# The layout of batch 0's inverse spectrum before its transposition by identity matmuls: strided or contiguous weight columns

## The chip, the cores and the metric

The kernel runs on one core of a Trainium2 chip. The metric is the device time of one execution in microseconds (us). The names are those of the profile: PE is TensorE's matmuls, PEld its weight loads (they overlap the matmuls: 432.1 and 322.8 us busy in a span of 441.9), DVE is VectorE, ACT ScalarE, POOL GpSimd. "Clock" is the share of TensorE's full clock that was granted, as the profile records it. "L617" is line 617 of the kernel; the change shortens the file by three lines, so L617 and L629 become L615 and L626 after it, and L660, L671, L704, L737, L740, L798, L1003, L1018 become L657, L668, L701, L734, L737, L795, L1000, L1015. ACT's evacuation stays L587.

In the kernel a matmul names a stationary operand, the weights, for which the profile has a weight load (LDWEIGHTS) of its own, and a moving operand. Its result goes to a PSUM tile (`ps` in the profile); an "evacuation" is the copy from there by ACT or DVE into a tile in SBUF, from which later matmuls read.

## The reference

A spectral layer and then a two-layer MLP whose weights are chosen per batch item:

```python
X = np.fft.rfft(x, axis=1)                    # x: 8 x 2496 x 256
Yr = Xr @ w_r - Xi @ w_i + b_r                # and Yi likewise
Yr = np.sign(Yr) * np.maximum(np.abs(Yr) - 0.01, 0.0)
y = np.fft.irfft(Yr + 1j * Yi, n=2496, axis=1)
# ... (one expert per batch item, from the mean of y)
h = np.maximum(y @ w1[e], 0.0); out = gate * (h @ w2[e])
```

The transforms are two-stage: 2496 = 39 x 64, so there are 64-point stages on 128 partitions and 39-point stages on 117 or 120. Between the two inverse stages the data changes its layout: 20 frequencies k and 128 positions n = (g, q), six q to each of 22 groups g, have to become 22 tiles with the 120 pairs (k, q) on partitions. Batches 1 to 7 do this through DRAM. Batch 0, which nothing can hide, does it on chip: it keeps the spectrum with channels on partitions and transposes it with 44 identity matmuls (22 groups, two channel halves). This change is about those.

## The kernel before

The instructions of all engines are emitted in an order that a small list scheduler in the kernel fixes when it is built. PE's instructions come in that order in the timelines, and while one waits no later one runs: in the last experiment below PE stood idle for 2.68 us before its first identity matmul.

The evacuation of the first inverse stage (L587) puts batch 0's spectrum into one tile `A`, for each half h as `(k, q, g)` with g innermost; positions 126 and 127 of each k go to a small zero-padded region, `first["r"]`, which serves as group g = 21.

```python
def add_inverse_b0(q, i0, n, cell, oy, vt):
    # ... matmuls L576: the 64-point inverse stage of n frequencies, into a PSUM pair
    def ev(eng):
        pv = hc["p"].rearrange("p h (k n) -> p h k n", k=n)
        k0 = 4 * q + i0
        COPY[eng](out=first["V"][:, :, 126 * k0 : 126 * (k0 + n)].rearrange(   # L587
            "p h (k q g) -> p h k q g", k=n, q=6),
            in_=pv[:, :, :, 0:126].rearrange("p h k (g q) -> p h k q g", q=6))
        COPY[eng](out=first["r"][...], in_=pv[:, :, :, 126:P])                # L591
```

The turn then takes four groups at a time (L617). The stationary operand of each matmul is 120 columns of `A`, 21 elements apart; the moving operand is the 128-column identity.

```python
def add_turn(v_ops, vt):
    for gq in range(6):
        gs = range(4 * gq, min(4 * gq + 4, NG))
        tag = "oh"[gq % 2]              # two PSUM pairs, used in turn
        def mm(_, ...):
            for i, g in enumerate(gs):
                for ch in range(2):
                    c0 = D * i + P * ch
                    nc.tensor.matmul(                                          # L617
                        pt[0:120, c0 : c0 + P],
                        first["V"][:, ch, g : g + 2500 : 21]
                        if g < 21 else first["r"][:, ch], eye)
        # ... evacuation of the pair to V2 by ACT or DVE (L629)
```

Between the six groups the scheduler puts the last inverse stage of batch 0 (L1003, evacuated by L1018) and work of batch 1 (L704, L737, L740). After the last of them comes L798, the first matmul of batch 2; from there on PE has work all the time. In what follows "the turn" is the stretch from the first identity matmul to the first L798 (L795 after the change).

## Time and profile before

| | before |
|---|---|
| time, median of 3 runs | 442.82 us (441.03 to 443.32) |
| the profiled execution | 443.56 us, span 441.9 us, mean clock 0.988 |
| the turn in it | 36.74 to 54.74 us: 18.00 us |

From the page of the profiled execution: the span, each engine's busy time (share of the span), the clock in 40 slices, in tenths, and the share of each engine in the chain of work that ended last.

```profile
span 441.9 us, 9430 instructions
...
PE 432.1 (98%) x3572; PEld 322.8 (73%) x3572; DVE 302.0 (68%) x616; ACT 333.1 (75%) x643; POOL 33.5 (8%) x54
...
PEclk9998699999999999999999999999999999999999
...
PE 92%; DMA 2%; DVE 2%; ACT 1%; SPq 1%; issue 1%; POOL 0%; ACTq 0%; POOLq 0%
```

PE sets the pace. The fourth and fifth slices of the clock line show the one flaw, at 33 to 55 us: 8 and 6 tenths. The table of windows for stretches of the turn and for all that follows it:

```profile
core 0: us, PE busy (x) PEld busy (x) DVE busy (x) ACT busy (x) POOL busy (x), PEclk, DMA share, GB/s
36.74:54.74 18.00, 17.57 (x113) 15.24 (x109) 7.35 (x8) 9.24 (x11) 0.00 (x0) 0.72 0.39 54
39.34:42.75 3.41, 3.41 (x14) 2.46 (x14) 0.66 (x1) 1.33 (x2) 0.00 (x0) 0.50 0.91 139
42.75:46.17 3.42, 3.42 (x25) 3.42 (x25) 1.23 (x1) 1.63 (x2) 0.00 (x0) 1.00 0.05 8
46.17:52.99 6.82, 6.82 (x44) 5.59 (x42) 3.05 (x3) 3.47 (x4) 0.00 (x0) 0.50 0.00 1
54.74:441.91 387.17, 383.55 (x3222) 289.12 (x3221) 274.28 (x553) 300.33 (x598) 23.00 (x34) 1.00 0.76 179
```

The window that follows the turn has PE busy for 383.55 of 387.17 us at full clock, so the end follows the start of that window, and what shortens the turn shortens the kernel. In the turn the clock is 0.50 in two stretches, 39.34 to 42.75 and 46.17 to 52.99 us: 3.41 us and twice that.

Next the weight loads of the turn, as the timeline shows them (start, duration of the merged group, engine, line, operation, operands, shapes, count):

```profile
36.69 1.85 PEld L617 LDWEIGHTS <-A 128*120 128x120 f16 x8
...
38.65 1.85 PEld L617 LDWEIGHTS <-A 128*120 128x120 f16 x8
...
44.19 1.86 PEld L617 LDWEIGHTS <-A 128*120 128x120 f16 x8
```

Eight loads take 1.85 us. A single one is recorded with 319 ns (median), so their spacing is about (1.85 - 0.32) / 7 = 0.22 us. The starts of the individual records say 222 ns. A matmul of 128 columns whose weights are ready needs only about 56 ns: eight L576 matmuls take 0.45 us in the chain. So in these groups PE has always something in flight, but by this estimate it computes only for 56 / 222, a quarter, of the time.

The same stretch on PE; the two groups below at 40.49 and 48.44 us ran at half clock:

```profile
36.74 1.94 PE L617 MATMUL ps<-eye,A 128*120 128x128 f16 x8
...
40.49 1.91 PE L704 MATMUL ps<-w,XB 128*128 128x512 f16 x4
...
48.44 0.99 PE L1003 MATMUL ps<-wi,V 120*128 120x117 f16 x8
...
50.94 0.73 PE L617 MATMUL ps<-eye,A 128*120 128x128 f16 x4
...
54.74 0.38 PE L798 MATMUL ps<-xin,wa 117*120 117x512 f16 x1 [0.43 <-ACT ysb L1018]
```

### The profile page before, as it was taken

To read this page: it belongs to the slowest core of one execution; us is meant where nothing else is said; L and a number is where in the kernel's file an instruction comes from. 1 tells how busy PE (TensorE), PEld (TensorE's weight loads), DVE (VectorE), ACT (ScalarE), POOL (GpSimd) and SP (SyncE) were. 2 spreads that over 40 slices of the span, in tenths; PEclk is the share of its full clock that TensorE was granted. 3 is DMA by queue.
4 is the path that set the end of the run, shared out by engine and by line. 5 is a ranking of instruction groups with operands and counts; after the bars stand their busy time and mean duration, and the time that the engine had idled before them with its cause. 6 is when DMAs were issued, how large, how long until landed. Compare 5 with 4: busy or idle time off the path is not lost.

```text
span 441.9 us, 9430 instructions
## 1 busy us (share of the span) xinstructions
PE 432.1 (98%) x3572; PEld 322.8 (73%) x3572; DVE 302.0 (68%) x616; ACT 333.1 (75%) x643; POOL 33.5 (8%) x54
## 2 busy tenths in 40 slices
PE   6999999999999999999999999999999999999996
PEld 2568866778777787778777787778777787777775
DVE  1484577487877869676877869677877869613662
ACT  3586598778777788667876788777876787778884
POOL 3230010020000210020000210020000010000000
PEclk9998699999999999999999999999999999999999
DMA  8899048979997799949987799959988368432122
GB/s 176 219 167 152 3 85 225 244 190 200 142 282 234 145 202 223 271 132 218 168 238 243 154 232 192 250 157 215 195 222 241 121 123 160 146 97 89 49 96 92
DMA packets 85605, 77.20 MB, mean 175 GB/s; under 512 B 7610, under 2 KB 72398, under 8 KB 85560
## 3 DMA queue, kind: packets, MB, share of 16 engines
q1 hardware_dynamic: 68366, 57.73, 47.5%
q0 software_dynamic: 16880, 18.46, 27.5%
q8 instruction: 28, 0.46, 0.4%
q10 hardware_dynamic: 314, 0.41, 0.3%
q14 instruction: 17, 0.14, 0.1%
HBM read 57.54 MB, written 37.49 MB: 215 GB/s over the span
## 4 chain that ended last, share of the span: by engine, by line
PE 92%; DMA 2%; DVE 2%; ACT 1%; SPq 1%; issue 1%; POOL 0%; ACTq 0%; POOLq 0%
PE ps L1305 30%; PE ps L1342 29%; PE ps L900 9%; PE ps L1045 4%; PE ps L529 3%; PE ps L798 3%; PE ps L704 3%; PE ps L862 3%; PE ps L1224 2%; PE ps L617 2%; DMA xin<-in_x_dram 2%; PE ps L737 1%; DMA ti<-d_ti 1%; PE ps L740 1%; PE ps L1003 1%; DVE z L752 1%
## 5 line engine op out<-in xcount | busy, mean ns | idle before, releaser
L1317 ACT ACTIVATE hs<-ps 128x512 f16<-128x512 f32 (+1 forms) x293 | 168.2, 594 | 68.2 <-PE ps L1305 64.2
L1305 PE MATMUL ps<-ysb,w1s 128*128 128x512 f16 (+1 forms) x640 | 178.2, 374 | 0.0
L1342 PE MATMUL ps<-w2s,hs 128*128 128x256 f16 x1152 | 162.3, 272 | 0.1
L1342 PEld LDWEIGHTS <-hs 128*128 128x128 f16 x1152 | 110.9, 98 | 42.7 <-issue 0.2
L1305 PEld LDWEIGHTS <-w1s 128*128 128x128 f16 x640 | 68.6, 113 | 18.6 <-issue 0.2
L914 DVE TENSOR_TENSOR tt<-ps,bias 128x512 f16<-128x512 f32 x60 | 38.6, 686 | 24.5 <-PE ps L900 24.5
L942 DVE TENSOR_TENSOR Y<-z,cl 64x512 f16<-64x512 f16 x120 | 50.4, 420 | 2.8
L900 PE MATMUL ps<-w,XT 128*128 128x256 f16 x360 | 49.4, 273 | 0.0
L1359 ACT ACTIVATE ost<-ps,gbc 128x512 f32<-128x512 f32 x65 | 44.7, 688 | 2.3 <-PE ps L1342 2.3
L900 PEld LDWEIGHTS <-XT 128*128 128x128 f16 x360 | 35.2, 98 | 7.7
L923 DVE TENSOR_TENSOR z<-ps,tt 128x512 f16<-128x512 f32 x60 | 38.4, 681 | 0.1
L808 ACT CAST A<-ps 120x512 f16<-120x512 f32 x48 | 29.5, 614 | 7.2 <-PE ps L798 6.8
L1061 DVE CAST ysb<-ps 128x468 f16<-128x468 f32 (+1 forms) x24 | 15.0, 630 | 25.6 <-PE ps L1045 25.5
L1061 ACT CAST ysb<-ps 128x468 f16<-128x468 f32 (+1 forms) x60 | 28.0, 523 | 3.2 <-PE ps L1045 2.6
L870 DVE CAST XT<-ps 128x512 f16<-128x512 f32 x24 | 16.5, 688 | 16.0 <-PE ps L862 16.0
L536 ACT CAST V<-ps 128x512 f16<-128x512 f32 x45 | 26.2, 609 | 0.0
L798 PE MATMUL ps<-xin,wa 117*120 117x512 f16 x66 | 23.1, 380 | 0.4 <-ACT ysb L1018 0.4
L1045 PE MATMUL ps<-wi,V 120*128 120x117 f16 (+1 forms) x308 | 22.4, 214 | 0.0
L870 ACT CAST XT<-ps 128x512 f16<-128x512 f32 x36 | 22.0, 615 | 0.0
L704 PE MATMUL ps<-w,XB 128*128 128x512 f16 x80 | 21.8, 404 | 0.1
L529 PE MATMUL ps<-Y,ti 128*128 128x256 f16 x140 | 21.8, 272 | 0.0
L536 DVE CAST V<-ps 128x512 f16<-128x512 f32 x25 | 17.2, 688 | 6.4 <-PE ps L529 5.4
(104 smaller groups left out, 438.4 us busy)
## 6 DMA issues: line engine op xcount, KB each, us to landing
out_dram<-ost SPq DMA_DIRECT2D x72, 256.0 KB
xin<-in_x_dram POOLq DMA_DIRECT2D x21, 429.0 KB, 11.7
scr<-V SPq DMA_DIRECT2D x35, 256.0 KB
XB<-fwd SPq DMA_DIRECT2D x30, 256.0 KB
V<-scr SPq DMA_DIRECT2D x14, 504.0 KB
fwd<-A SPq DMA_DIRECT2D x18, 360.0 KB
w1s<-in_moe_w_dram POOLq DMA_DIRECT2D x8, 512.0 KB, 7.4
w2s<-in_moe_w_dram POOLq DMA_DIRECT2D x8, 512.0 KB, 8.0
```

The lines of the kernel that those rows point to most:

```text
L536: COPY[eng](out=hc["V"][:, n * u : n * u + n].rearrange("p i c -> p (i c)"), in_=hc["p", u])
L870: COPY[eng](out=cell["X"][:, ch, :, 0:2].rearrange("p a r i k -> p a i r k"), in_=hc["p"].rearrange("p (a i r k) -> p a i r k", a=2, i=2, ...
L900: nc.tensor.matmul(pm[:, D * a : D * a + D], cell["X"][:, ch, a, t].rearrange("p i k -> p (i k)"), w4[:, ch, t, :], start=(ch == 0), stop= ...
L914: nc.vector.tensor_add(out=cell["tt"][:, r], in0=cell["T", 2].rearrange("p (a c) -> p a c", a=2), in1=bias[:, r].unsqueeze(1).to_broadcast ...
L923: nc.vector.tensor_add(out=cell["z"][:, r], in0=cell["T", 1 - r].rearrange("p (a c) -> p a c", a=2), in1=cell["tt"][:, r])
L942: nc.vector.tensor_sub(out=Y[64 * r : 64 * r + 64, :, i], in0=cell["z"][s, r], in1=cell["cl"][s, r])
L1045: nc.tensor.matmul(pi[:, 117 * i : 117 * i + M], V2[:, g, ch * P : ch * P + P], w)
L1061: COPY[eng](out=yv[:, :, 12 * gb : 12 * gb + 3 * nf].rearrange("p a (g j) -> p a g j", j=3), in_=pi[:, 0 : 117 * nf].rearrange("p (g a j) ...
L1305: nc.tensor.matmul(ph[:, 0:nl], w1v[:, ch, fc // 4, :, fc % 4], ysb_t[b][:, ch, ns : ns + nl], start=(ch == 0), stop=(ch == 1))
L1317: nc.scalar.activation(out=o, in_=i, func=AFT.Relu)
L1342: nc.tensor.matmul(oc["p"][:, i, :], cell["hs"][:, ft, s0 : s0 + P], w2s_t[b][:, ft, :], start=(ft == 0), stop=(ft == E - 1))
L1359: nc.scalar.activation(out=ost, in_=oc["p"], func=AFT.Copy, scale=gbc_t[b])
```

## The change

The evacuation now writes each group's 120 columns next to each other: layout `(g, k, q)` with q innermost, and group 21 as one more g. The loads become contiguous. The evacuation reads PSUM contiguously and writes runs of six fp16 values (12 bytes) 240 bytes apart; before it wrote runs of 504.

```diff
-                first["V"] = A[:, 0 : 252 * NK1].rearrange(
-                    "p (h m) -> p h m", h=2)
-                first["r"] = A[:, 252 * NK1 : 264 * NK1].rearrange(
-                    "p (h m) -> p h m", h=2)
-                nc.vector.memset(A[:, 252 * NK1 : 264 * NK1], 0.0)
+                first["V"] = V = A[:, 0 : 240 * NG].rearrange(
+                    "p (h g k q) -> p h k g q", h=2, g=NG, q=6)
+                first["T"] = A[:, 0 : 240 * NG].rearrange(
+                    "p (h g m) -> p h g m", h=2, g=NG)
+                nc.vector.memset(V[:, :, :, 21], 0.0)
...
-            COPY[eng](out=first["V"][:, :, 126 * k0 : 126 * (k0 + n)].rearrange(
-                "p h (k q g) -> p h k q g", k=n, q=6),
-                in_=pv[:, :, :, 0:126].rearrange(
-                "p h k (g q) -> p h k q g", q=6))
-            COPY[eng](out=first["r"][:, :, 6 * k0 : 6 * (k0 + n)].rearrange(
-                "p h (k q) -> p h k q", k=n)[:, :, :, 0:2],
-                in_=pv[:, :, :, 126:P])
+            COPY[eng](out=first["V"][:, :, k0 : k0 + n, 0:21],
+                      in_=pv[:, :, :, 0:126].rearrange(
+                          "p h k (g q) -> p h k g q", q=6))
+            COPY[eng](out=first["V"][:, :, k0 : k0 + n, 21, 0:2],
+                      in_=pv[:, :, :, 126:P])
...
-                            first["V"][:, ch, g : g + 2500 : 21]
-                            if g < 21 else first["r"][:, ch], eye)
+                            first["T"][:, ch, g], eye)
```

No computing instruction is added or dropped, and their order on every engine is the same.

## The prediction

> **What bounds the kernel now.** From about 56 us on PE never stops: the table of windows shows it 100% busy at clock 1.00. The end follows the start of that dense run, the first L798 matmul (54.74 us in the timeline). From 36.74 to there runs batch 0's tail: six groups of identity matmuls (L617, 44 in all), in fixed PE order with L1003, L704, L737/740. The chain of waits there is almost all PE, 10 us of it L617.
>
> **Why L617 is slow.** Its weight loads take 319 ns (median), one every 222 ns, at full and half clock alike; their columns lie 42 bytes apart. Loads with contiguous columns take 98 ns (128 columns) and 133 ns (120 columns, L798). A control: the last two weights (g=21) are contiguous already; their spacing is 80 to 107 ns at half clock. [...]
>
> **Second cost.** Slow loads leave PE computing a quarter of the time, and the granted clock falls to 0.50 at 39.2 to 42.7 and 46.2 to 53.0 us. There four L704 matmuls cost 1.71 instead of 0.86 us (twice), eight L1003 0.79 instead of 0.42. [...]the trace's steps are 3.41 us.
>
> **What the change does.** Removes the stride from 42 of 44 loads; instruction counts and order stay. It moves the scatter to ACT's evacuation L587: PSUM read becomes contiguous, SBUF writes become runs of 6 fp16 (12 bytes) 240 bytes apart, formerly 504 contiguous.
>
> **Sum (estimates from the durations above).** Spacing 222 to about 56 ns: 42 x 0.166 = 7.0 us of PE. Clock staying at 1.0: about 3 us more. Given back: PE then waits for evacuations (two pairs of banks; 1.0 us on ACT, 1.2 on DVE) and for the shared rings. Replaying the fixed order with these durations, L798 starts near 46.1: 8.6 us gained, bounded at the end by ACT's evacuations of L1003.
> Cost: ACT evacuations with short scattered runs are slower in this trace: runs of 3 elements (39 of them) cost 0.37 us against 0.26 expected by count, single elements 0.39 against 0.19, about 5 ns per jump; runs of 12 cost nothing. Runs of 6 last 5 ns, so just about hidden[...]. I give 20% to a clock drop remaining (costs 1 to 3 us).
> Net gain: about 7.7 us, all on the critical path, as PE runs dense afterwards.
>
> **Prediction: 435.0 us, 8 in 10 between 432.8 and 438.0.** Faster by over 2% (below 433.96): 0.27; within 2%: 0.72; slower: 0.01.
>
> **What would show it.** L617 loads near 133 ns, spacing near 56; window 36 to 47 at clock 1.00; L617's part of the chain about 2.5 us, not 10; first L798 near 46 to 47.5; PE waits released by ACT or DVE evacuations; L587 1.0 to 1.4 us; from L798 to the end unchanged (387 us).
>
> **What would make it wrong.** Scattered writes slower than 1.4 us; the clock dropping anyway; L798's input landing after 46 us (it landed about 44 to 45).

The sum came to about 7.7 us net: 7.0 us from the loads and about 3 from the clock, of which the replay with its waits left 8.6, less the costs weighed by their chances. One of these costs: a slower evacuation L587 (about 1 us, at 35%). The 0.9 us between 8.6 and 7.7 contains that term, and the 1.4 us among the criteria was its upper end. That the slow loads lower the clock was the estimate here; an experiment below tests it.

## The result, and the profile after

| | before | after |
|---|---|---|
| first comparison, median | 442.07 us (441.03 to 443.32, 4 runs) | 435.67 us (435.40 to 435.87, 4 runs) |
| ratio, 95% interval | | 0.9854 (0.9823 to 0.9885) |
| repeated with more rounds, median | 443.06 us (440.91 to 444.98, 11 runs) | 435.53 us (435.30 to 435.81, 6 runs) |
| ratio, 95% interval | | 0.9833 (0.9804 to 0.9862) |

A ratio here is the mean time of one kernel's fast runs over that of the other's of the same rounds, so it is not quite the ratio of the medians in the table. The gain is 1.5 to 1.7%, clear of noise and short of 2%.

The page after, the same lines:

```profile
span 434.1 us, 9428 instructions
...
PE 423.7 (98%) x3572; PEld 314.9 (73%) x3572; DVE 301.9 (70%) x616; ACT 332.7 (77%) x643; POOL 33.1 (8%) x54
...
PEclk9999999999999999999999999999999999999999
...
PE 93%; DVE 3%; ACT 2%; issue 1%; ACTq 0%
```

The clock line has no dip any more. The weight loads of the turn:

```profile
37.38 0.52 PEld L615 LDWEIGHTS <-A 128*120 128x120 f16 x8
...
38.23 0.52 PEld L615 LDWEIGHTS <-A 128*120 128x120 f16 x8
...
40.66 0.52 PEld L615 LDWEIGHTS <-A 128*120 128x120 f16 x8
```

Eight loads in 0.52 instead of 1.85 us; one takes 133 ns, and the spacing of the individual records is 56 ns, that of the matmuls themselves. PE in the turn:

```profile
37.43 0.61 PE L615 MATMUL ps<-eye,A 128*120 128x128 f16 x8
...
38.98 1.04 PE L701 MATMUL ps<-w,XB 128*128 128x512 f16 x4
...
42.22 0.58 PE L1000 MATMUL ps<-wi,V 120*128 120x117 f16 x8
...
43.66 0.39 PE L615 MATMUL ps<-eye,A 128*120 128x128 f16 x4
...
46.86 0.38 PE L795 MATMUL ps<-xin,wa 117*120 117x512 f16 x1 [0.43 <-ACT ysb L1015]
```

The turn starts at 37.43 and ends at 46.86 us, 9.43 us long instead of 18.00. (It started 0.69 us later than in the profiled execution of before. That shift stands already at 21 us, before the first changed instruction: an ACT cast that began at 21.01 us in the one began at 21.70 in the other, and near 9 us DVE had waited 7.87 instead of 7.16 us for the first input. It belongs to the execution, not to the change.) The windows:

```profile
core 0: us, PE busy (x) PEld busy (x) DVE busy (x) ACT busy (x) POOL busy (x), PEclk, DMA share, GB/s
37.43:46.86 9.43, 8.63 (x112) 6.90 (x109) 7.25 (x8) 8.75 (x11) 0.00 (x0) 1.00 0.78 99
46.86:434.10 387.24, 383.57 (x3222) 289.13 (x3221) 274.31 (x553) 300.43 (x598) 22.67 (x34) 1.00 0.74 179
```

The rest of the kernel takes 387.24 us, where it took 387.17: nothing was given back later. But in the turn PE now has pauses. The chain of waits has pieces of ACT and DVE between those of PE (start, length, what):

```profile
37.63 0.46 ACT XB L668
38.09 0.40 issue
38.49 0.44 ACT XB L668
...
43.82 0.24 PE ps L615 x4
44.06 0.02 issue
44.08 0.70 DVE V L626
...
45.42 0.43 PE ps L1000 x8
45.85 0.02 issue
45.87 0.95 ACT ysb L1015
```

In the profiled execution of before, the only such piece in the turn was the last one, ACT's evacuation L1018, for which the first L798 waits (0.43 us). But that execution was slowed by its clock: in the one at full clock that is shown below, the chain has DVE's piece of 0.70 us as well. New with the fast loads are only the two pieces of ACT's L668.

The evacuation L587 that now scatters its writes, before and then after (count, duration in ns as min/median/max, first and last start, shapes):

```profile
L587 ACT CAST A<-ps x6: 578/1002/1054, 23.3 to 35.8; 128x1008 f16<-128x1008 f32 x4, 128x504 f16<-128x504 f32 x2
```

```profile
L587 ACT CAST A<-ps x6: 690/1020/1077, 24.0 to 36.4; 128x1008 f16<-128x1008 f32 x4, 128x504 f16<-128x504 f32 x2
```

### The profile page after: what moved, and what is told of

Its sections match the earlier page's. It is cut to its first block, busy times and chain, and to the rows that moved or that the text cites. A ratio compares the mean times of both kernels' runs of the same rounds, so it can differ in the third digit from the quotient of the medians.

```text
span 434.1 us, 9428 instructions
## 1 busy us (share of the span) xinstructions
PE 423.7 (98%) x3572; PEld 314.9 (73%) x3572; DVE 301.9 (70%) x616; ACT 332.7 (77%) x643; POOL 33.1 (8%) x54
## 4 chain that ended last, share of the span: by engine, by line
PE 93%; DVE 3%; ACT 2%; issue 1%; ACTq 0%
PE ps L1302 31%; PE ps L1339 29%; PE ps L897 9%; PE ps L1042 4%; PE ps L529 4%; PE ps L795 3%; PE ps L859 3%; PE ps L701 3%; PE ps L1221 2%; PE ps L441 2%; DVE z L749 1%; PE ps L734 1%; PE ps L657 1%; PE ps L737 1%; DVE Y L764 1%
## 5 line engine op out<-in xcount | busy, mean ns | idle before, releaser
L867 DVE CAST XT<-ps 128x512 f16<-128x512 f32 x24 | 16.5, 688 | 16.0 <-PE ps L859 16.0
L795 PE MATMUL ps<-xin,wa 117*120 117x512 f16 x66 | 23.1, 380 | 0.4 <-ACT ysb L1015 0.4
L1042 PEld LDWEIGHTS <-V 120*128 120x128 f16 x308 | 19.8, 98 | 2.4
```

Of the source, the lines that this page charges most:

```text
L867: COPY[eng](out=cell["X"][:, ch, :, 0:2].rearrange("p a r i k -> p a i r k"), in_=hc["p"].rearrange("p (a i r k) -> p a i r k", a=2, i=2, ...
L1042: nc.tensor.matmul(pi[:, 117 * i : 117 * i + M], V2[:, g, ch * P : ch * P + P], w)
```

## The experiments

Seven kernels. The theory, an estimate from the profile of before: the gain has two parts, the loads themselves (PE waits for weights, one load every 222 ns) and the clock (it falls to 0.50 because PE waits). The rivals: the clock is only a symptom; or the scatter of the kernel before has another source, so that the clock part was misread.

### The kernel before once more

No edit.

> The unchanged kernel once more, to see its own scatter. Theory 'clock phase': [...]its executions differ (441.0 to 443.3 us so far) and the longer ones have the lower mean granted clock; ratio 1.00, another profile with the half-clock stretches begun at another point of the turn and the turn (first L617 to first L798) 16.5 to 18.5 us long. Rival 'input landing': the scatter is in the first 20 us (landing of x), and the turn is 18.0 us again to 0.1 us.

Measured: 443.08 us median (440.95 to 444.46, 6 runs), ratio 1.0008 (0.9975 to 1.0042). The profiled execution was the fastest of the six, 440.95 us, and in it the clock never fell:

```profile
36.72 1.94 PE L617 MATMUL ps<-eye,A 128*120 128x128 f16 x8
...
40.46 1.03 PE L704 MATMUL ps<-w,XB 128*128 128x512 f16 x4
...
47.34 0.58 PE L1003 MATMUL ps<-wi,V 120*128 120x117 f16 x8
...
48.62 0.55 PE L617 MATMUL ps<-eye,A 128*120 128x128 f16 x4
...
51.99 0.38 PE L798 MATMUL ps<-xin,wa 117*120 117x512 f16 x1 [0.43 <-ACT ysb L1018]
```

```profile
36.72:51.99 15.27, 14.64 (x112) 13.53 (x109) 7.35 (x8) 9.12 (x11) 0.00 (x0) 1.00 0.47 59
```

The first fence is PE in the turn, the second the window of the turn. The same program, the same loads, but L704 at 40.46 takes 1.03 instead of 1.91 us, L1003 at 47.34 takes 0.58 instead of 0.99, and the turn is 15.27 us long instead of 18.00. The profiles agree up to the first group's start (36.72 and 36.74 us). So the turn missed my 16.5 to 18.5 us: I had expected the dips to move, and in this execution there was none at all. What holds of the theory is that the longer executions are those with the lower clock, as the table below shows. The half-clock stretches can lie differently: the longer one begins at 46.17 us in before, and at about 44.6 us in the second kernel with other steps below, which is the same up to the turn (there the group of L1002 at 44.57 takes 0.97 us, where the one at 42.49 takes 0.58). What decides where they lie and how many there are is not shown.

For 25 executions of before the mean granted clock is on record (the 11 of these rounds, these six, seven of the experiments, and the first profiled one). One stretch of 3.41 us at half clock lowers the mean over 442 us by 0.5 x 3.41 / 442 = 0.004; the profiled execution, with three times 3.41 us at 0.50, has a mean of 0.988. By this estimate the recorded clock tells how many such stretches there were, from none in the first line to four in the last:

| mean clock | executions | time, mean (range) |
|---|---|---|
| 0.999 to 1.000 | 6 | 441.3 us (440.91 to 442.00) |
| 0.995 | 4 | 442.2 us (442.05 to 442.45) |
| 0.991 to 0.992 | 5 | 443.4 us (443.06 to 444.00) |
| 0.988 | 9 | 444.0 us (443.56 to 444.98) |
| 0.983 | 1 | 444.46 us |

The rival "input landing" explains a scatter of 0.7 us or so in the first 37 us of the profiles, not this order of 3 us by clock.

### The strided loads with a busier PE

```diff
                     c0 = D * i + P * ch
+                    w = (512 - c0 % 512) // P
                     nc.tensor.matmul(
-                        pt[0:120, c0 : c0 + P],
+                        pt[0:120, c0 : c0 + P * w].rearrange("p (w c) -> p w c", w=w),
                         first["V"][:, ch, g : g + 2500 : 21]
-                        if g < 21 else first["r"][:, ch], eye)
+                        if g < 21 else first["r"][:, ch],
+                        eye.unsqueeze(1).to_broadcast([P, w, P]))
```

> Strided weights as before, but every identity matmul streams 1 to 4 copies of the identity (320 columns on average), whose extra output is overwritten by the next ones; result right. Spacing stays 222 ns, PE computes about 60% of it instead of 25%. Theory 'two costs': the clock stays at 1.00 in the turn and about 3 us of the gain come without touching the loads: 438.5 to 440 us, ratio about 0.993. Rival 'the loads are all': the clock is a symptom and worth nothing: ratio 1.000. If the clock falls all the same, the run tells nothing.

Measured: 441.49 us median (441.25 to 441.80, 6 runs), result right, ratio 0.9966 (0.9936 to 0.9996). The recorded clock was 0.999 to 1.000 in all six, where before in the same rounds ranged from 0.988 to 1.000. Its turn, at full clock:

```profile
37.47:52.95 15.48, 14.70 (x112) 13.69 (x109) 7.35 (x8) 9.13 (x11) 0.00 (x0) 1.00 0.47 60
```

This answers two questions. Adding useless columns, and nothing else, stops the dips (0.999 or more in all six, where 8 of the 11 executions of before had 0.988 to 0.995), so in these runs the dips came from how little PE computed while it waited for weights; and stopping them makes the kernel faster on average, by just more than the noise, and takes away its scatter. The clock is not a mere symptom. But the gain is 1.5 us (0.34%), not the 3 us that I had put down, because only some executions of before had lost 3 us. The turn is as long as that of the undisturbed execution of before (15.48 and 15.27 us): the strided loads alone keep it there.

### The contiguous loads with the old evacuation

```diff
-                            first["V"][:, ch, g : g + 2500 : 21]
+                            first["V"][:, ch, 120 * g : 120 * g + 120]
                             if g < 21 else first["r"][:, ch], eye)
```

The result is wrong: the loads read whatever 120 neighbours lie there.

> The evacuation of before (contiguous writes), but the identity matmuls read 120 contiguous columns of it: wrong data on purpose. Theory 'the loads are the whole gain and the scattered writes cost nothing': the same time as the changed kernel within 0.3 us (about 435.6). Rival 'the writes take a part back': 0.5 to 1.5 us faster than the changed kernel, L587 at 1.00 us against 1.02.

Measured: 435.28 us median (435.08 to 435.84, 6 runs), ratio 0.9830 (0.9800 to 0.9859). L587 has a median of 1.00 us here, and the turn takes 9.43 us, exactly as in the changed kernel. So the gain is in the loads. No cost of the scattered writes is shown: the two medians differ by 0.25 us, and the ranges of the two kernels overlap. (The old evacuation also reads PSUM with a step of six values, which the new one does not; the runs compare both together.)

### The changed kernel in the same rounds

> The changed kernel in the same rounds, as the mark for the others: ratio 0.985 (0.982 to 0.988), turn 9.4 us, clock 1.00, spread of its runs under 1 us where before has 2 us.

Measured: 435.53 us median (435.30 to 435.81, 6 runs), ratio 0.9833 (0.9804 to 0.9862), turn 37.05 to 46.48 us (9.43 us), clock 0.999 to 1.000 in all six. As expected; the scatter of before is gone.

### Which steps between columns are slow

Two kernels with before's evacuation, where each of the six groups of loads reads its columns with another step (the edit is abbreviated). Wrong results on purpose, and one look each (437.95 and 442.14 us, single executions that mix the steps; only the durations of the loads are used).

```diff
-                            first["V"][:, ch, g : g + 2500 : 21]
-                            if g < 21 else first["r"][:, ch], eye)
+                            first["V"][:, ch, g % 16 : g % 16 + 119 * s[gq] + 1 : s[gq]], eye)
                             # s = (2, 3, 4, 5, 8, 16) in one, (6, 7, 9, 10, 12, 20) in the other
```

> Before's evacuation; the six groups of identity matmuls read weights whose 120 columns lie 2, 3, 4, 5, 8, 16 fp16 apart (4, 6, 8, 10, 16, 32 bytes), one step a group; wrong data on purpose. [...] Rival 'any step is slow': about 222 ns at every step. Rival 'the cost grows with the distance': under 222 ns at step 8 and 16.

> The same with steps 6, 7, 9, 10, 12, 20 (12 to 40 bytes). [...] Any step is slow: all 222. Grows with the distance: a rise from 9 to 20.

The weight loads of the first of the two kernels, eight each with steps 2, 3, 4, 5 and 8, and, as the last line, the eight with step 12 of the second:

```profile
37.10 0.54 PEld L617 LDWEIGHTS <-A 128*120 128x120 f16 x8
...
37.95 0.76 PEld L617 LDWEIGHTS <-A 128*120 128x120 f16 x8
...
39.35 1.07 PEld L617 LDWEIGHTS <-A 128*120 128x120 f16 x8
...
40.77 1.19 PEld L617 LDWEIGHTS <-A 128*120 128x120 f16 x8
...
42.30 1.83 PEld L617 LDWEIGHTS <-A 128*120 128x120 f16 x8
...
45.24 1.78 PEld L617 LDWEIGHTS <-A 128*120 128x120 f16 x8
```

The usual spacing of the loads in a group, from the starts of the individual records (step 1 from the changed kernel, step 21 from before):

| step, fp16 | 1 | 2 | 3 | 4 | 5 | 6 | 7 | 8 | 9 | 10 | 12 | 16 | 20 | 21 |
|---|---|---|---|---|---|---|---|---|---|---|---|---|---|---|
| bytes | 2 | 4 | 6 | 8 | 10 | 12 | 14 | 16 | 18 | 20 | 24 | 32 | 40 | 42 |
| spacing, ns | 56 | 56 | 85 | 111 | 140 | 167 | 193 | 220 | 213 | 206 | 209 | about 220 | 212 to 218 | 222 |

The two fall in the form in which I wrote them: "any step is slow" falls at step 2 (56 ns), "grows with the distance" falls above step 8 (220 ns there, 206 to 222 beyond). What fits these groups is simpler: up to step 8, columns 16 bytes apart, the spacing grows in proportion to the step, and beyond it stays about the same. A price of 27.6 ns per step gives 83, 110, 138, 166, 193, 221 ns for s = 3 to 8, within 3 ns of the usual spacings in the table. At step 2 it gives 55 ns, just hidden behind the matmul's 56. That price is a fit to these groups, not something the trace records, and what causes it is not shown. Why steps 9 to 12 are a few per cent under the plateau stays open. In before the spacing of the loads was the same at full and at half clock (median 222 ns in the group at 44.19 us, 223 in the one at 46.58), so here it did not follow the granted clock.

### Writes without runs

The changed kernel with (q, k) for (k, q) in the 120 columns, and the rows of the inverse table in the same order, so that the result is right and the loads are contiguous:

```diff
-    wi0 = wi.transpose(1, 0, 2).reshape(120, 117)
+    wi0 = wi.reshape(120, 117)
...
-                    "p (h g k q) -> p h k g q", h=2, g=NG, q=6)
+                    "p (h g q k) -> p h k g q", h=2, g=NG, q=6)
```

> The changed kernel, with the 120 columns of a weight in the other order (q slow, k fast) and the inverse table to match: result right, loads contiguous as in the changed kernel (56 ns), but ACT's evacuation writes single fp16 values 40 and 240 bytes apart instead of runs of 6. Theory 'ACT pays about 5 ns per jump, hidden under runs of 6': L587 about 5 us for 1008 elements instead of 1.02, and the kernel 10 to 16 us slower than the changed one (445 to 452 us). Rival 'scattered writes are free for ACT here': L587 1.0 us and 435.5 us.

Measured: 453.14 us median (453.02 to 453.29, 4 runs), ratio 1.0221 (1.0189 to 1.0252): slower than before, though unclear at 2%, because the interval lies on both sides of it. By the medians it is 17.6 us slower than the changed kernel, more than the 10 to 16 us expected. It was run at another time. The evacuation, and the start of the turn (L590 is the second copy of the same evacuation):

```profile
L587 ACT CAST A<-ps x6: 2383/4580/4616, 23.8 to 50.3; 128x1008 f16<-128x1008 f32 x4, 128x504 f16<-128x504 f32 x2
...
53.08 1.11 PE L615 MATMUL ps<-eye,A 128*120 128x128 f16 x8 [2.68 <-ACT A L590]
```

4.58 us instead of 1.02 for 1008 values. A copy of 1024 values takes 1.01 us on ACT and one of 512 takes 0.61, so 0.2 us are fixed and a value costs 0.78 ns; here it costs (4.58 - 0.2) / 1008 = 4.3 ns. The turn starts at 53.08 us, 16 us later than in the changed kernel, because PE waits for these evacuations, and while it waits the clock falls too (mean 0.976 to 0.981), which my estimate had left out: the turn begins at half clock and takes 11.11 us, to 64.19 us, instead of 9.43. So the loads could have been made contiguous in a way that loses more than it gains. By these numbers runs of six are just long enough: 1008 values in runs of six are 168 jumps, 168 x 4.3 ns = 0.72 us, less than the 0.79 us (1008 x 0.78 ns) that ACT needs for the values anyway. That the jumps hide behind the values in this way is an estimate from these durations. A copy in runs of three that every one of these kernels has agrees with it: 234 values (the last of L1018, 78 runs) take 0.52 us, where the values alone would give 0.2 + 234 x 0.78 ns = 0.38 us and the jumps 0.2 + 78 x 4.3 ns = 0.54.

## Why the prediction was right

It said 435.0 us, 432.8 to 438.0, with 72% for "within 2%"; measured were 435.67 and 435.53 us, 1.5 to 1.7% faster.

- **What bounds the kernel.** Right. The part after the turn took 387.17 us before and 387.24 after, and the gain is that of the turn.
- **The loads.** Right, also in size. Spacing 222 to 56 ns, 133 ns for one. Undisturbed by the clock, the turn went from 15.27 to 9.43 us: 5.84 us. The 42 loads that lost their stride would account for 42 x 0.166 = 6.97 us. Two of them, each the first after a group of L704, were hidden before already (in the undisturbed execution their matmuls are followed by the next after 59 ns), so 40 x 0.166 = 6.64 us could be gained; the other 0.8 us became pauses of PE.
- **The pauses.** Right. The replay of the fixed order gave 46.1 - 36.74 = 9.4 us for the turn; measured are 9.43. The chain shows ACT's and DVE's evacuations as the releasers, though DVE's was there before at full clock too. In these 9.43 us ACT is busy for 8.75 and DVE for 7.25 us, so that a still faster PE would probably gain little here; no run tested that.
- **The clock.** Right that it would stay up (0.999 to 1.000 in all six runs), mis-sized. "About 3 us more" was read off one profiled execution that had three times 3.41 us at half clock, one of the longer ones of the table above (443.56 us). There it is 18.00 - 15.27 = 2.73 us. But executions of before had, by the estimate above, between none and about four such stretches, and the mean loss is smaller: 442.9 us (the time after, 435.5, over the ratio 0.9833) less 441.3 is 1.6 us in the repeated comparison, and 442.1 - 441.3 = 0.8 us in the first. This is why the measured gain, 6.4 us by the first medians, is less than the 7.7 predicted; in the repeated comparison it was 7.5. (The sums close: 5.84 + 0.8 = 6.6 and 5.84 + 1.6 = 7.4.) That 7.7 came so close to 7.5 is partly luck. The replay's 8.6 us was right for the one execution that it was read from, whose turn the change shortened by 18.00 - 9.43 = 8.57 us; the 0.9 us between it and the net 7.7, put down to costs that then did not come, stood in for the 1.1 us (2.73 - 1.6) that an average execution had not lost. I had seen the scatter of 2.3 us in three runs and not asked whether it was the same thing.
- **The evacuation.** The favourable one of the two cases that I had left open: 1.02 us. The other, up to 1.4 us, did not come; nor did the 20% for a clock that drops all the same.
- **The input of batch 2** was there in time: the wait before L795 is for ACT's evacuation (0.43 us), as before.

What is not settled: when the clock falls. The runs show only that with PE computing a quarter of the time in the groups of loads (by estimate) it fell in 19 of 25 executions (mean 0.995 or less), and that with about 60% (by estimate: 320 columns of 2.5 x 56 ns in 222 ns) it did not in six. A PE that is busy by the profile did not keep it up: in before PE and PEld were busy for 3.42 of 3.42 us from 42.75 to 46.17 us, and the 6.82 us that follow ran at 0.50.

## What to carry to other kernels

In these runs the spacing of weight loads of 120 fp16 columns followed the step between the columns, so look at that step for every stationary operand: 56 ns at steps 1 and 2, 85 already at step 3, and 206 to 222 from step 8 on, nearly four matmuls of 128 columns (220 to 56 ns). Loads of 128 columns, which take 98 ns when contiguous here (L1342) against 133 for 120 (L798), were not tried with a step. When a layout has to change, let the side pay that has the time, and keep its runs long enough: six fp16 values cost ACT's writes nothing that shows (1.02 us), single ones 4.5 times the copy (4.58 us). And before taking the price of a lowered clock from one trace, look at the clocks of several executions: the 25 of before had means from 0.983 to 1.000.
